# Blocked decay attention and a squared-ReLU feed-forward: block sums of the second products on VectorE with due times, all squares on ScalarE, two visits placed otherwise

## The chip, the cores and the metric

The kernel runs on one core of one Trainium2 chip. A core has TensorE (PE in the profile; its weight loads are PEld), VectorE (DVE), ScalarE (ACT), GpSimd (POOL) and SyncE (SP), which issues the transfers here. The metric is the device time of one execution in microseconds.

## The reference

Four batches of eight heads, 768 positions, head dimension 64. Attention without softmax, in blocks of 64 positions with a state; the result, 3072 tokens by 512, goes through a feed-forward of width 2048 with a squared ReLU:

```python
intra = np.einsum('bhic,bhjc->bhij', qb, kb) * Dmask[None]
intra = np.einsum('bhij,bhjd->bhid', intra, vb)
inter = np.einsum('bhid,bhde->bhie', qb * lam_pow[None], kv_state)
out[:, :, sl] = intra + inter
kv_state = lam_block[None, :, None, None] * kv_state + np.einsum('bhsd,bhse->bhde', kb_dec, vb)
...
h = np.maximum(x @ w_in, 0.0)
return (h * h @ w_out).astype(np.float32)
```

## The kernel before

**Tiles and twins.** The tokens are 24 chunks of 128. The first eight form three tiles (3, 3 and 2 chunks; `SIZES`), whose feed-forward is done step by step over 16 blocks of the width (`ffn`): every fp32 factor is split into a rounded high half and a low half, and three matmuls stand for one. The other 16 chunks form two twins of eight chunks, 512 columns wide twice. Their feed-forward multiplies 2 x 2 blocks with seven products instead of eight (a Strassen scheme in Winograd's form).

**First products.** `first_products` does, for each of eight pairs `j` of width blocks, the seven products of x with blocks of w_in; a product is six matmuls of 512 columns. ScalarE copies three of them out of PSUM (`copy`, L865), VectorE adds (`block`, L869), ScalarE applies the ReLU (L870), and the square is made on VectorE for `t == 0` (L872), on ScalarE otherwise (L874). The four results of a pair, h(t, f), are 512 columns each.

**Second products.** `second_products` goes through the seven products in the order 4, 1, 2, 6, 5, 7, 3 (`LAST_ORDER`), eight times each (a pass). Each product splits its block of h: ScalarE rounds the high half (L916), VectorE subtracts it for the low half (L917). Products 6, 5, 7 and 3 use sums of blocks; these four sums per pair are made in place on GpSimd (`add`, L923) once the earlier products have read the blocks (`sums_of`). VectorE and ScalarE collect results (L953, L956, L982). All operations of a twin's second products carry one due time, `key`, but for the splits.

**Weights.** `differences` makes the sums of weight blocks on GpSimd (L795, L804), splits them (L807 on ScalarE, L808 on VectorE) and stores them to memory; `streamed` loads 256 KB of them for each product (L844).

**Visits.** The attention of later chunks is done two chunks at a time in visits, put between the steps and products by the tables `VISITS`, `BETWEEN` (after which step of tile 2) and `INSIDE` (before which product of twin 0). A visit has a first half, an opening, a second half and another opening; between the halves a one-column copy (L684) orders the two. `PARTED` names the piece after which a visit is cut, with pieces of a step in between. After a visit, `pairs` makes sums and splits of x for the twins (L821 ScalarE, L822 VectorE; the sums at L830 on VectorE for the last pair of twin 0, on GpSimd for the others).

**What sets the order.** `Plan.order` lists all operations with a cost and a due time for each and writes out one fixed order per engine: an engine takes, of the operations that could start now, the one with the smallest due time. Each engine then works through its list in order. TensorE's order in the twins is linked by hand (`link`).

Of the kernel before, what the change touches and what calls it, by code (L numbers as in the profile page):

```python
# [226 lines left out]
PARTED = {2: 2, 5: 1}  # L227
BETWEEN = {3: 3, 4: 10, 5: 12}
# [50 lines left out]
def kernel(ctx: ExitStack, tc: tile.TileContext, ka, qv, lamx, w, out):  # L279
# [533 lines left out]
    def pairs(p, j, chunks2, key):  # L813
# [13 lines left out]
        def add(out_, a, b, op, deps):  # L827
            part = lambda c: at(c[0])[:, c[1]]
            eng, dur, fn = (("DVE", tt(256), nc.vector), ("POOL", 0.84, nc.gpsimd))[p or j < 3]
            return [plan.op(eng, dur, key, lambda: fn.tensor_tensor(out=part(out_), in0=part(a), in1=part(b), op=op), deps, [xa_, xb_])]  # L830
# [10 lines left out]
    def streamed(i, j, k, key):  # L841

        b = Buf("b")
        return b, plan.op("SP", LOAD, key - 12, lambda: nc.sync.dma_start(out=at(b).bitcast(F32), in_=kept[i][j][:, :, KEPT[k]]), stored[i, j], [b], lat=3.2)  # L844

    def first_products(p, j, key):
# [20 lines left out]
        def block(k, t, f, a, deps):  # L867
# [32 lines left out]
    def second_products(p, key):  # L900
# [6 lines left out]
        names = [f"end{k}" for k in range(4)] + ["ob9"]  # L907

# [12 lines left out]
        def add(j, out_, a, b, op, deps):  # L921
            o, a, b = ((t, 2 * j + e) for t, e in (out_, a, b))
            made[o] = [plan.op("POOL", 1.38, key, lambda: nc.gpsimd.tensor_tensor(out=at(h[o]), in0=at(h[a]), in1=at(h[b]), op=op), deps + made[a] + made[b], [h[o], h[a], h[b]])]  # L923

        def sums_of(i, j):
            if i == 4:
                add(j, (1, 1), (1, 0), (1, 1), ALU.add, read[4, j])
                add(j, (1, 0), (0, 0), (1, 0), ALU.subtract, made[1, 2 * j + 1])
            if i == 1:
                add(j, (0, 0), (1, 1), (0, 0), ALU.subtract, read[1, j] + made[1, 2 * j])  # L930
            if i == 2:
                add(j, (0, 1), (0, 1), (0, 0), ALU.subtract, read[2, j])
# [19 lines left out]
        def copies(i, dst):  # L952
            return [plan.op("ACT", act(WIDE) + 0.09, key, lambda a=a, b=b: nc.scalar.copy(at(a), at(b)), [last[i]], [a, b], uses=names) for a, b in zip(dst, banks[i])]  # L953
# [248 lines left out]
```

## Time and profile before

| | |
|---|---|
| median of 3 runs | 607.9 us (607.8 to 610.38) |
| profiled execution | 606.75 us, its span 605.0 us |
| busy, PE / PEld | 574.2 us (95%) / 471.4 us (78%) |
| busy, DVE / ACT / POOL | 470.9 us (78%) / 320.4 us (53%) / 237.7 us (39%) |
| granted clock, mean | 0.986 |
| q1 (all loads and stores) | 136.34 MB, 71.6% of 16 engines |

A busy share is an average over stages that differ. The stages, in us from the span's start: tiles 0 and 1 to about 176, tile 2 to about 249, twin 0 from 245 to 439 (first products, then from 341 second products), twin 1 from 439 to 601 (second products from 514). In a row of the timeline, equal instructions that follow each other are merged with their count; an engine is busy from the first to the last. TensorE's matmuls overlap, so a row's length is a little over the distance to the next row's start, and that distance is what one product costs.

### The profile page before, as it was taken

The numbers are of one execution on the slowest core, as the hardware profiler recorded it, in microseconds if no ns is written. First come the engines' busy times: TensorE is split into PE (matmuls) and PEld (weight loads), VectorE is DVE, ScalarE is ACT, GpSimd is POOL, SyncE is SP. The second block draws the span as 40 slices with busy tenths as digits, with TensorE's granted clock in tenths as the row PEclk, the third lists the DMA queues.
The fourth block names the chain that finished last, engine by engine and source line by source line (L and its number), as shares of the span: only waits on it lengthen the run. The fifth ranks groups of instructions, "written<-read, shape, count | busy, mean of one in ns | idle before, by whom it ended". The sixth has DMA issues, their size and how long they took to land.

```text
span 605.0 us, 12945 instructions
## 1 busy us (share of the span) xinstructions
PE 574.2 (95%) x4917; PEld 471.4 (78%) x4917; DVE 470.9 (78%) x710; ACT 320.4 (53%) x660; POOL 237.7 (39%) x198
## 2 busy tenths in 40 slices
PE   9999999999999998899989969999999999999997
PEld 7798899998878887678868757667888888666786
DVE  6998999955894879676795999998543446999755
ACT  5776677653544554457557434464345465543442
POOL 3000000042774647146662699991000002999200
PEclk9999999999998998899999979999999999999999
DMA  8999799827774692699999516566886766655765
GB/s 343 346 333 277 245 296 292 301 87 249 249 246 172 244 286 90 205 295 315 311 363 297 155 45 178 155 204 163 244 246 194 194 195 194 172 155 142 211 196 185
DMA packets 104398, 137.18 MB, mean 227 GB/s; under 512 B 7056, under 2 KB 88976, under 8 KB 104336
## 3 DMA queue, kind: packets, MB, share of 16 engines
q1 hardware_dynamic: 104192, 136.34, 71.6%
q8 instruction: 39, 0.64, 0.4%
q14 instruction: 23, 0.19, 0.1%
q10 hardware_dynamic: 144, 0.01, 0.0%
HBM read 100.67 MB, written 35.65 MB: 225 GB/s over the span
## 4 chain that ended last, share of the span: by engine, by line
PE 66%; DVE 18%; DMA 9%; issue 3%; ACT 1%; POOL 1%; SPq 1%; DVEq 0%; POOLq 0%; ACTq 0%
PE bank L469 45%; PE bank L738 9%; DVE v L917 6%; PE bank L747 4%; PE bank L744 4%; PE bank L745 4%; DMA b<-kept 3%; DMA ka<-ka 2%; DMA qv<-qv 2%; DVE gl L756 1%; DMA out<-ob 1%; DMA work<-w 1%; DVE pt L822 1%; DVE hold L553 1%; DVE h L872 1%
## 5 line engine op out<-in xcount | busy, mean ns | idle before, releaser
L469 PE MATMUL bank<-v,b 128*128 128x512 f32 x672 | 168.3, 401 | 5.6 <-DVE v L917 4.0
L469 PEld LDWEIGHTS bank<-v,b 128*128 128x128 f32 x672 | 123.1, 189 | 49.8 <-DVE v L917 25.7
L923 POOL TENSOR_TENSOR h<-h,h 128x512 f32<-128x512 f32 x64 | 105.0, 1673 | 118.8 <-DVE v L917 114.2
L917 DVE TENSOR_TENSOR v<-h,v 128x512 fp32r<-128x512 f32 x112 | 125.8, 1167 | 17.4 <-ACT v L916 13.5
L916 ACT CAST v<-h 128x512 fp32r<-128x512 f32 x112 | 67.7, 621 | 73.9 <-PE bank L469 57.5
L869 DVE TENSOR_TENSOR h<-bank,u 128x512 f32<-128x512 f32 x64 | 43.8, 690 | 63.1 <-PE bank L469 30.0
L795 POOL TENSOR_TENSOR ob<-wi 128x512 f32<-128x512 f32 x16 | 22.0, 1390 | 149.9 <-DVE xa L756 118.9
L870 ACT ACTIVATE h<-h 128x512 f32<-128x512 f32 x64 | 40.3, 632 | 33.3 <-DVE h L869 31.8
L865 ACT COPY u<-bank 128x512 f32<-128x512 f32 x48 | 27.9, 581 | 44.6 <-PE bank L469 44.6
L469 PE MATMUL bank<-ps,b 128*128 128x512 f32 x192 | 49.3, 392 | 1.7 <-ACT h L870 1.5
L469 PE MATMUL bank<-pa,b 128*128 128x512 f32 x192 | 50.4, 399 | 0.4 <-DMA b<-kept 0.2
L744 PE MATMUL bank<-wo,gh 128*128 128x512 f32 x125 | 50.3, 402 | 0.4 <-issue 0.3
L745 PE MATMUL bank<-wo,gh 128*128 128x512 f32 x125 | 49.6, 397 | 1.1 <-issue 0.9
L469 PE MATMUL bank<-pt,b 128*128 128x512 f32 x192 | 46.7, 391 | 0.0
L469 PEld LDWEIGHTS bank<-ps,b 128*128 128x128 f32 x192 | 35.7, 188 | 10.5 <-ACT h L870 1.9
L469 PEld LDWEIGHTS bank<-pa,b 128*128 128x128 f32 x192 | 36.5, 192 | 9.2 <-DMA b<-kept 1.0
L469 PEld LDWEIGHTS bank<-pt,b 128*128 128x128 f32 x192 | 35.8, 188 | 8.1 <-issue 0.5
L795 POOL TENSOR_TENSOR ob<-wo 128x512 f32<-128x512 f32 x16 | 23.3, 1462 | 38.8 <-DVE v L808 30.7
L738 PE MATMUL bank<-xb,wi 128*128 128x384 f32 x192 | 35.2, 336 | 0.0
L804 POOL TENSOR_TENSOR ob<-ob,ob 128x256 f32<-128x256 f32 x40 | 33.1, 827 | 3.1
L738 PEld LDWEIGHTS bank<-xb,wi 128*128 128x128 f32 x192 | 33.6, 188 | 0.9
L738 PE MATMUL bank<-xa,wi 128*128 128x384 f32 x180 | 34.1, 338 | 0.0
(152 smaller groups left out, 1018.3 us busy)
## 6 DMA issues: line engine op xcount, KB each, us to landing
b<-kept SPq DMA_DIRECT2D x224, 256.0 KB, 3.4
work<-w SPq DMA_DIRECT2D x32, 512.0 KB, 4.6
ka<-ka SPq DMA_DIRECT2D x24, 512.0 KB, 5.4
qv<-qv SPq DMA_DIRECT2D x20, 512.0 KB, 5.8
kept<-part SPq DMA_DIRECT2D x32, 256.0 KB, 3.6
kept<-v SPq DMA_DIRECT2D x32, 256.0 KB, 4.1
kept<-wo SPq DMA_DIRECT2D x24, 256.0 KB, 3.5
kept<-wi SPq DMA_DIRECT2D x8, 512.0 KB, 4.2
```

Source lines behind the costliest of these rows:

```text
L469: nc.tensor.matmul(*args, **kw, skip_group_check=True)
L738: nc.tensor.matmul(at(h)[:, 0:n], wt[:, cc, :], xt[:, cc, :], start=k == 0, stop=k == 3 * NCC - 1)
L744: nc.tensor.matmul(at(os_[j]), at(gh)[:, sl], woh[f], start=f == 0 and ti >= SINGLE, stop=False)
L745: nc.tensor.matmul(at(os_[j]), at(gh)[:, sl], wol[f], start=False, stop=False)
L795: prev = [plan.op("POOL", 1.38, key, lambda r=r, a=a: nc.gpsimd.tensor_tensor(out=at(r), in0=a[:, 0].bitcast(F32), in1=a[:, 1].bitcast(F32 ...
L804: o = plan.op("POOL", 0.84, key, lambda out_=out_, a=a, b=b: nc.gpsimd.tensor_tensor(out=side(out_), in0=side(a), in1=side(b), op=ALU.subt ...
L865: return plan.op("ACT", act(WIDE) + 0.09, key - 6, lambda: nc.scalar.copy(at(dst), at(banks[k])), [o], [banks[k], dst])
L869: o = plan.op("DVE", tt(WIDE) + 0.1, key - 6, lambda: nc.vector.tensor_tensor(out=at(b), in0=at(banks[k]), in1=at(a), op=ALU.add), deps, [ ...
L870: o1 = plan.op("ACT", act(WIDE) + 0.12, key, lambda: nc.scalar.activation(at(b), at(b), AF.Relu), [o], [b])
L916: oh = plan.op("ACT", act(WIDE) + 0.12, key - 12, lambda: nc.scalar.copy(rounded[hi.slot], at(b)), made[t, 2 * j + e], [b, hi], after)
L917: ol = plan.op("DVE", tt(WIDE) + 0.1, key - 12, lambda: nc.vector.tensor_tensor(out=rounded[lo.slot], in0=at(b), in1=rounded[hi.slot], op= ...
L923: made[o] = [plan.op("POOL", 1.38, key, lambda: nc.gpsimd.tensor_tensor(out=at(h[o]), in0=at(h[a]), in1=at(h[b]), op=op), deps + made[a] + ...
```

## The change

The sums of h in the second products go from GpSimd to VectorE and get due times of their own, by the product that uses them (`user`); the collecting operations get the due time at which their pass ends (`ended`). All sums of x in `pairs` go to VectorE, with later due times. All squares are made on ScalarE. Streamed loads follow each other in the order of the program (`in_turn`). The differences of w_out are due earlier, and visit 4 stands after step 9 of tile 2 instead of 10 and is cut after its first opening.

```diff
-PARTED = {2: 2, 5: 1}
-BETWEEN = {3: 3, 4: 10, 5: 12}
+PARTED = {2: 2, 4: 1, 5: 1}
+BETWEEN = {3: 3, 4: 9, 5: 12}
...
-            eng, dur, fn = (("DVE", tt(256), nc.vector), ("POOL", 0.84, nc.gpsimd))[p or j < 3]
-            return [plan.op(eng, dur, key, lambda: fn.tensor_tensor(out=part(out_), in0=part(a), in1=part(b), op=op), deps, [xa_, xb_])]
+            return [plan.op("DVE", tt(256), key, lambda: nc.vector.tensor_tensor(out=part(out_), in0=part(a), in1=part(b), op=op), deps, [xa_, xb_])]
...
-        return b, plan.op("SP", LOAD, key - 12, lambda: ...
+        return b, in_turn("streamed", plan.op("SP", LOAD, key - 12, lambda: ...
...
-            if t == 0:
-                o1 = plan.op("DVE", tt(WIDE) + 0.1, key, lambda: nc.vector.tensor_tensor(out=at(b), in0=at(b), in1=at(b), op=ALU.mult), [o1], [b])
-            else:
-                o1 = plan.op("ACT", act(WIDE) + 0.12, key, lambda: nc.scalar.activation(at(b), at(b), AF.Square), [o1], [b])
+            o1 = plan.op("ACT", act(WIDE) + 0.12, key, lambda: nc.scalar.activation(at(b), at(b), AF.Square), [o1], [b])
...
+        def ended(i):
+            return start + PASS * LAST_ORDER.index(i)
...
-        def add(j, out_, a, b, op, deps):
+        def add(j, user, out_, a, b, op, deps):
+            when = start + PASS * LAST_ORDER.index(user) + A_PROD * j - 14
             o, a, b = ((t, 2 * j + e) for t, e in (out_, a, b))
-            made[o] = [plan.op("POOL", 1.38, key, lambda: nc.gpsimd.tensor_tensor(out=at(h[o]), in0=at(h[a]), in1=at(h[b]), op=op), deps + made[a] + made[b], [h[o], h[a], h[b]])]
+            made[o] = [plan.op("DVE", tt(WIDE) + 0.1, when, lambda: nc.vector.tensor_tensor(out=at(h[o]), in0=at(h[a]), in1=at(h[b]), op=op), deps + made[a] + made[b], [h[o], h[a], h[b]])]
...
-            pairs(p - len(SIZES), j // 2, old, key if p == len(SIZES) else twice[0][1] + 4 + 12 * (j // 2))
+            pairs(p - len(SIZES), j // 2, old, begin[2] + per[2] * (11 + j / 2) if p == len(SIZES) else twice[0][1] + 30 + 8 * (j // 2))
...
-            differences(i, j, 480 + 9 * j if i == 0 else 700 + 9 * j)
+            differences(i, j, 480 + 9 * j if i == 0 else 618 + 6 * j)
```

The order that comes of it, at three places. Some line numbers are one lower in the changed program: a split's low half stands at L916, a block's addition at L868, a pair sum at L829; the sum of h is L923 in both.

VectorE, before, from the last block addition of twin 0 to the first one-column copy (L684) of the last visit; `h` are blocks of h, `v` the halves of splits, `pa` and `pz` sums of x for twin 1:

```order
L869 TENSOR_TENSOR h_0_196<-bank_58,u_214 128x512
L917 TENSOR_TENSOR v_227<-h_0_202,v_226 128x512
L917 TENSOR_TENSOR v_222<-h_0_206,v_225 128x512
L872 TENSOR_TENSOR h_0_196<-h_0_196 128x512
L917 TENSOR_TENSOR v_224<-h_0_208,v_223 128x512
L822 TENSOR_TENSOR pa<-xr_117,pa 128x4x128
L917 TENSOR_TENSOR v_227<-h_0_210,v_226 128x512
L822 TENSOR_TENSOR pz<-work,pz 128x2x128
L684 COPY small<-bank_62 128x1
```

And VectorE, changed, the same place:

```order
L923 TENSOR_TENSOR h_0_204<-h_0_203,h_0_204 128x512
L923 TENSOR_TENSOR h_0_203<-h_0_187,h_0_203 128x512
L868 TENSOR_TENSOR h_0_196<-bank_63,u_218 128x512
L916 TENSOR_TENSOR v_224<-h_0_202,v_225 128x512
L916 TENSOR_TENSOR v_226<-h_0_206,v_221 128x512
L923 TENSOR_TENSOR h_0_202<-h_0_201,h_0_202 128x512
L916 TENSOR_TENSOR v_228<-h_0_208,v_223 128x512
L923 TENSOR_TENSOR h_0_201<-h_0_185,h_0_201 128x512
L916 TENSOR_TENSOR v_225<-h_0_210,v_224 128x512
L923 TENSOR_TENSOR h_0_206<-h_0_205,h_0_206 128x512
L684 COPY small<-bank_62 128x1
```

The splits of x and the square behind the last addition are gone from here, and five sums of h (L923) stand ahead of the copy.

VectorE, before, the first splits of the second products of twin 1:

```order
L917 TENSOR_TENSOR v_227<-h_0_198,v_221 128x512
L917 TENSOR_TENSOR v_228<-h_0_200,v_223 128x512
L872 TENSOR_TENSOR h_0_195<-h_0_195 128x512
L869 TENSOR_TENSOR h_0_212<-bank_65,u_218 128x512
L869 TENSOR_TENSOR h_0_211<-bank_60,u_218 128x512
L917 TENSOR_TENSOR v_222<-h_0_204,v_224 128x512
L869 TENSOR_TENSOR h_0_196<-bank_65,u_217 128x512
L917 TENSOR_TENSOR v_227<-h_0_202,v_226 128x512
L917 TENSOR_TENSOR v_225<-h_0_206,v_221 128x512
L872 TENSOR_TENSOR h_0_196<-h_0_196 128x512
L917 TENSOR_TENSOR v_228<-h_0_208,v_223 128x512
L917 TENSOR_TENSOR v_227<-h_0_210,v_226 128x512
```

And VectorE, changed:

```order
L916 TENSOR_TENSOR v_225<-h_0_198,v_221 128x512
L916 TENSOR_TENSOR v_224<-h_0_200,v_226 128x512
L923 TENSOR_TENSOR h_0_198<-h_0_197,h_0_198 128x512
L923 TENSOR_TENSOR h_0_200<-h_0_199,h_0_200 128x512
L923 TENSOR_TENSOR h_0_197<-h_0_181,h_0_197 128x512
L923 TENSOR_TENSOR h_0_199<-h_0_183,h_0_199 128x512
L868 TENSOR_TENSOR h_0_212<-bank_65,u_214 128x512
L868 TENSOR_TENSOR h_0_211<-bank_64,u_214 128x512
L916 TENSOR_TENSOR v_223<-h_0_204,v_227 128x512
L923 TENSOR_TENSOR h_0_204<-h_0_203,h_0_204 128x512
L923 TENSOR_TENSOR h_0_203<-h_0_187,h_0_203 128x512
L868 TENSOR_TENSOR h_0_196<-bank_65,u_220 128x512
```

Four sums of h stand behind the first two splits, and then one or two ahead of each further one; the squares (L872) are gone.

TensorE, before, step 11 and the start of step 12 of tile 2 (`wi`, `wo` are weights, `gh` and `gl` the halves of h in a tile), ahead of visit 4:

```order
L738 MATMUL bank_58<-x_131,wi_77 128x256 x12
L744 MATMUL bank_60<-wo_92,gh_0_102 128x512
L745 MATMUL bank_60<-wo_92,gh_0_102 128x512
L744 MATMUL bank_65<-wo_92,gh_0_102 128x512
L745 MATMUL bank_65<-wo_92,gh_0_102 128x512
L747 MATMUL bank_60<-wo_92,gl_0_104 128x512
```

And TensorE, changed, between the two parts of visit 4; the rows on `qv`, `ka` and `work` are the visit's:

```order
L469 MATMUL bank_59<-qv_110,ka_108 64x64 x2
L744 MATMUL bank_60<-wo_92,gh_0_102 128x512
L745 MATMUL bank_60<-wo_92,gh_0_102 128x512
L744 MATMUL bank_65<-wo_92,gh_0_102 128x512
L745 MATMUL bank_65<-wo_92,gh_0_102 128x512
L738 MATMUL bank_61<-x_131,wi_77 128x256 x12
L469 MATMUL bank_58<-work,qv_111 64x64 x2
L469 MATMUL bank_63<-work 64x64 x2
```

The first part of visit 4 now stands ahead of the high halves of one step and the first product of the next, and its second part ahead of that step's low half.

## Rows read from the trace of the kernel before

**Rows 1.** Stages: span; busy PE, PEld, DVE, ACT, POOL (instructions); clock, DMA share, GB/s.
```profile
217.10:249.40 32.30, 26.59 (x597) 22.87 (x597) 30.74 (x52) 14.86 (x37) 17.75 (x18) 0.89 0.49 161
249.40:340.93 91.53, 88.35 (x1062) 71.97 (x1060) 68.70 (x113) 50.94 (x109) 48.40 (x46) 1.00 0.92 296
340.93:358.61 17.68, 11.06 (x160) 8.23 (x158) 16.72 (x18) 8.28 (x18) 14.04 (x9) 0.87 0.38 108
358.61:438.93 80.32, 77.71 (x315) 57.91 (x313) 71.74 (x75) 38.06 (x66) 49.42 (x35) 0.99 0.63 179
438.93:516.62 77.69, 77.69 (x343) 64.11 (x342) 35.33 (x51) 42.35 (x75) 5.86 (x4) 1.00 0.72 203
516.62:601.36 84.74, 82.71 (x331) 59.74 (x329) 69.67 (x64) 36.77 (x62) 47.49 (x29) 1.00 0.62 178
```

**Rows 2.** Timeline of TensorE, first products of twin 1: start, us, instruction, count.
```profile
458.14 1.52 PE L469 MATMUL bank<-ps,b 128*128 128x512 f32 x6
459.50 1.52 PE L469 MATMUL bank<-pa,b 128*128 128x512 f32 x6
```

**Rows 3.** Chain that ended last, second products of twin 0: start, us, what.
```profile
376.62 1.65 PE bank L469 x6
378.31 1.65 PE bank L469 x6
```

**Rows 4.** Timeline, second products of twin 0, GpSimd and VectorE.
```profile
364.40 28.57 POOL L923 TENSOR_TENSOR h<-h,h 128x512 f32<-128x512 f32 x17 [1.56 <-DVE v L917]
...
366.29 28.38 DVE L917 TENSOR_TENSOR v<-h,v 128x512 fp32r<-128x512 f32 x17
```

**Rows 5.** Timeline of VectorE before the twins, with GpSimd idle.
```profile
226.79 0.67 DVE L578 TENSOR_TENSOR xr<-bank,rdec 128x512 f32<-128x512 f32 x1
227.39 0.68 DVE L822 TENSOR_TENSOR ps<-xk,ps 128x512 fp32r<-128x512 f32 x1
227.99 0.41 DVE L822 TENSOR_TENSOR pz<-work,pz 128x256 fp32r<-128x256 f32 x1
228.32 0.41 DVE L553 TENSOR_TENSOR hold<-hold,small 128x256 f32<-128x256 f32 x1
```

**Rows 6.** Groups by line: count | busy us, mean ns | idle before, what ended it.
```profile
L917 DVE TENSOR_TENSOR v<-h,v 128x512 fp32r<-128x512 f32 x112 | 125.8, 1167 | 17.4 <-ACT v L916 13.5 <-PE bank L469 3.9
...
L923 POOL TENSOR_TENSOR h<-h,h 128x512 f32<-128x512 f32 x64 | 105.0, 1673 | 118.8 <-DVE v L917 114.2 <-issue 4.4
...
L872 DVE TENSOR_TENSOR h<-h 128x512 f32<-128x512 f32 x32 | 30.0, 936 | 1.4 <-ACT h L870 0.7
...
L874 ACT ACTIVATE h<-h 128x512 f32<-128x512 f32 x32 | 18.2, 616 | 0.0
...
L830 DVE TENSOR_TENSOR xk<-xk,xk 128x256 f32<-128x256 f32 x2 | 0.8, 418 | 0.0
```

**Rows 7.** Timeline of TensorE, last visit; in brackets idle time and its releaser.
```profile
349.61 0.46 PE L469 MATMUL bank<-s,qv 64*64 64x64 f32 x16
...
350.61 0.28 PE L469 MATMUL bank<-s,qv 64*64 64x64 f32 x4
355.88 0.58 PE L469 MATMUL bank<-s,qv 64*64 64x64 f32 x10 [4.99 <-DVE small L684]
```

**Rows 8.** Timeline of VectorE around the last visit.
```profile
332.44 1.29 DVE L917 TENSOR_TENSOR v<-h,v 128x512 fp32r<-128x512 f32 x2
...
350.94 1.75 DVE L822 TENSOR_TENSOR pa<-xr,pa 128x512 fp32r<-128x512 f32 x1
```

**Rows 9.** Chain that ended last: a visit and two steps of tile 2.
```profile
192.94 3.89 PE bank L469 x240
...
208.71 1.43 PE bank L738 x12
211.53 1.43 PE bank L738 x12
```

**Rows 10.** Waits of the weight loads, 210 to 250 us: us in total, times, longest.
```profile
PEld bank L747 <- DVE gl L756: 5.5, 2, 3.2
```

More of the change, by code (lines that the diff above doesn't have):

```diff
@@ L843, in streamed @@
         b = Buf("b")
-        return b, plan.op("SP", LOAD, key - 12, lambda: nc.sync.dma_start(out=at(b).bitcast(F32), in_=kept[i][j][:, :, KEPT[k]]), stored[i, j], [b], lat=3.2)
+        return b, in_turn("streamed", plan.op("SP", LOAD, key - 12, lambda: nc.sync.dma_start(out=at(b).bitcast(F32), in_=kept[i][j][:, :, KEPT[k]]), stored[i, j], [b], lat=3.2))
     def first_products(p, j, key):
@@ L898, in first_products, with second_products @@
         return run
-    def second_products(p, key):
+    def second_products(p, start):
         h, made = hidden[p], ready_h[p]
@@ L919, in splits @@
             return hi, lo, oh, ol
-        def add(j, out_, a, b, op, deps):
+        def add(j, user, out_, a, b, op, deps):
+            when = start + PASS * LAST_ORDER.index(user) + A_PROD * j - 14
             o, a, b = ((t, 2 * j + e) for t, e in (out_, a, b))
-            made[o] = [plan.op("POOL", 1.38, key, lambda: nc.gpsimd.tensor_tensor(out=at(h[o]), in0=at(h[a]), in1=at(h[b]), op=op), deps + made[a] + made[b], [h[o], h[a], h[b]])]
+            made[o] = [plan.op("DVE", tt(WIDE) + 0.1, when, lambda: nc.vector.tensor_tensor(out=at(h[o]), in0=at(h[a]), in1=at(h[b]), op=op), deps + made[a] + made[b], [h[o], h[a], h[b]])]
         def sums_of(i, j):
             if i == 4:
-                add(j, (1, 1), (1, 0), (1, 1), ALU.add, read[4, j])
-                add(j, (1, 0), (0, 0), (1, 0), ALU.subtract, made[1, 2 * j + 1])
+                add(j, 6, (1, 1), (1, 0), (1, 1), ALU.add, read[4, j])
+                add(j, 6, (1, 0), (0, 0), (1, 0), ALU.subtract, made[1, 2 * j + 1])
             if i == 1:
-                add(j, (0, 0), (1, 1), (0, 0), ALU.subtract, read[1, j] + made[1, 2 * j])
+                add(j, 6, (0, 0), (1, 1), (0, 0), ALU.subtract, read[1, j] + made[1, 2 * j])
             if i == 2:
-                add(j, (0, 1), (0, 1), (0, 0), ALU.subtract, read[2, j])
+                add(j, 3, (0, 1), (0, 1), (0, 0), ALU.subtract, read[2, j])
         def product(i, j, key):
@@ L952, in copies @@
         def copies(i, dst):
-            return [plan.op("ACT", act(WIDE) + 0.09, key, lambda a=a, b=b: nc.scalar.copy(at(a), at(b)), [last[i]], [a, b], uses=names) for a, b in zip(dst, banks[i])]
+            return [plan.op("ACT", act(WIDE) + 0.09, ended(i), lambda a=a, b=b: nc.scalar.copy(at(a), at(b)), [last[i]], [a, b], uses=names) for a, b in zip(dst, banks[i])]
         def plus(i, dst, src, deps):
-            return [plan.op("DVE", tt(WIDE) + 0.1, key, lambda a=a, b=b, c=c: nc.vector.tensor_tensor(out=at(a), in0=at(b), in1=at(c), op=ALU.add), [last[i], o] + more, [a, b, c], uses=names)
+            return [plan.op("DVE", tt(WIDE) + 0.1, ended(i), lambda a=a, b=b, c=c: nc.vector.tensor_tensor(out=at(a), in0=at(b), in1=at(c), op=ALU.add), [last[i], o] + more, [a, b, c], uses=names)
                     for a, b, c, o, more in zip(dst, banks[i], src, *deps)]
@@ L961, in store @@
                 n = N_PLAIN + 8 * p + 4 * t + 2 * d + k
-                plan.op("SP", 1.0, key, lambda a=a, n=n: nc.sync.dma_start(out=out[n], in_=at(a)), [o], [a], uses=names)
+                plan.op("SP", 1.0, start, lambda a=a, n=n: nc.sync.dma_start(out=out[n], in_=at(a)), [o], [a], uses=names)
         def after(i):
@@ L981, in after @@
                 st["r3"] = copies(7, st["a7"])
-                o4 = [plan.op("DVE", tt(WIDE), key, lambda a=a, b=b: nc.vector.tensor_tensor(out=at(a), in0=at(a), in1=at(b), op=ALU.add), [x, y], [a, b], uses=names)
+                o4 = [plan.op("DVE", tt(WIDE), ended(7), lambda a=a, b=b: nc.vector.tensor_tensor(out=at(a), in0=at(a), in1=at(b), op=ALU.add), [x, y], [a, b], uses=names)
                       for a, b, x, y in zip(st["a4"], st["a7"], st["rz"], st["r3"])]
```

## The prediction

> **What bounds the kernel now.** I read the busy times by stage first [rows 1]: TensorE's six stretches from 217.10 us on, with the count of its matmuls. In the three that belong to the second products and to the step just before the twins, VectorE is busy 30.74 of 32.30, 16.72 of 17.68, 71.74 of 80.32 and 69.67 of 84.74 us, and GpSimd is busy too; in the first products of twin 1 (438.93 to 516.62) GpSimd rests, VectorE has 35.33 of 77.69 us, and TensorE never stops. Next I took the pitch of one product. Where nothing holds TensorE, two products of six matmuls start 1.36 us apart [rows 2]; in the second products they start 1.69 us apart [rows 3]. What sets 1.69 stands in the same stretch on two other engines: 17 GpSimd sums in 28.57 us and 17 VectorE splits in 28.38 us, 1.68 and 1.67 us each, in lockstep [rows 4]. Without GpSimd beside it VectorE starts a 512-wide instruction every 0.60 us and a 256-wide one every 0.33 us [rows 5], and the means of a whole program show the same: the split (L917) 1.167 us, the square on VectorE (L872) 0.936 us, against 0.418 us for the few 256-wide pair sums that VectorE makes already [rows 6]. So the second products are paced by VectorE and GpSimd slowing each other, not by TensorE.
>
> The time above the pure matmul time, stretch by stage:
> - 516.62 to 601.36 holds 55 products: 55 x 1.36 = 74.8 of 84.74 us, so 9.9 lost.
> - 358.61 to 438.93 holds 52: 70.7 of 80.32, so 9.6 lost.
> - 340.93 to 358.61 holds 5 products (6.8) and the last visit, whose matmuls take about 3.4 (1.3 up to 350.89 [rows 7] and 2.1 in two parts behind the copies): 10.2 of 17.68, so 7.5 lost. 4.99 of it is one wait for a one-column copy on VectorE (L684) [rows 7], which stands behind a queue of instructions at up to 1.75 us each [rows 8].
> - 217.10 to 249.40: a tile-2 step costs 2.82 us, of which 1.43 is its first product, and a visit about 3.9 [rows 9]. Four first parts, five second parts (1.39), two visits and one product are 5.7 + 7.0 + 7.8 + 1.4 = 21.9 of 32.30, so 10.4 lost: waits for the low half on VectorE (L756; 5.5 us on the weight loads [rows 10]) and TensorE at a granted 0.89, that is, partly at 1.2 GHz, after its pauses [rows 1].
>
> **The change, part by part.**
>
> *Sums of second products from GpSimd to VectorE.* 64 instructions leave GpSimd (1.673 us each, 105 us [rows 6]) and 64 of 512 columns come to VectorE. Before shows none of just this sum there; its nearest rows are the 512-wide instructions with two SBUF inputs without GpSimd, 0.60 us in a row. I take 0.60, the pitch of the nearest row; the bounds are 0 (all of them in VectorE's idle time) and 1.167, the split's mean beside GpSimd; with whole spans and no overlap it is 0.69 [rows 5]. Read from the order of the changed program, VectorE has in the last four fifths of twin 0's second products (from the last L684 on) 94 wide instructions (49 splits, 21 sums, 12 pair splits, 12 others) and 24 narrow: 94 x 0.60 + 24 x 0.335 = 64.5 us, beside 70.7 us of TensorE. In twin 1 it has 67 wide ones in the first four passes: 40.2 us beside 32 x 1.36 = 43.5. Both are below TensorE, by 9% and 8%, so TensorE sets the pace again if the order is smooth: a split may run some three products ahead, and the sums mostly stand singly between two splits. Where they come in fours (the start of twin 1: 11 sums and 3 block additions among 8 splits, 22 x 0.60 = 13.2 us against 10.9) a few products wait: I leave 1.5 us lost in each twin. Gain 80.32 - 70.7 - 1.5 = 8.1 for twin 0 and 84.74 - 74.8 - 1.5 = 8.4 for twin 1.
>
> The Trainium skill speaks against this part: Perfetto Trace Analysis, Optimizing Scalar/DVE Operations, advises taking work off a saturated VectorE, even to GpSimd, and adds that the two share a port, so that it might not help. By its first half the gain above would turn into the loss priced under the second rival; by its second half, which rows 4 bear out with 1.68 us, there is nothing to lose.
>
> *The last visit.* From the first split of twin 0 to the first L684 of this visit the order now has 21 wide and 8 narrow instructions: 12.6 + 2.7 = 15.3 us from 332.44 [rows 8], the later of them waiting for a block that TensorE finishes at about 343.7 (340.93 and two products); seven wide ones and two copies stand behind that block, which makes 349. TensorE gets there at 340.93 + 6.8 + 1.2 = 348.9. The wait of 4.99 us and the 1 us before it shrink to about 1.5: 10.2 + 1.5 = 11.7 instead of 17.68, gain 6.0. Bounds: 0 (if the burst of sums ahead of the copy costs as much as the contention did) and 7.5.
>
> *Squares to ScalarE.* 32 instructions of 0.936 us leave VectorE, 32 of 0.616 [rows 6] come to ScalarE. In the first products ScalarE goes from 42.35 to 42.35 + 16 x 0.616 = 52.2 of 77.69 us (twin 1) and from 50.94 to 60.8 of 91.53 (twin 0) [rows 1]. Not on the path: cost 0, bounds 2 lost and 2 won (twin 0 loses about 6 us in that stretch now: 54 x 1.36 and three visits of 3.9 make 85.1 of 91.53; its transfers, which the change leaves as they are, are the nearest cause: 296 GB/s at a DMA share of 0.92 [rows 1]).
>
> *Pair sums to VectorE, with due times, and visit 4 a step earlier and parted.* 28 narrow sums move. 16 are counted above. The other 12 fall into the stretch before the twins: VectorE has there, from the first pair split to the first block, 20 wide and 45 narrow instructions, 27.1 us without GpSimd, where before 21 wide and 34 narrow (24.0 us by the same pitch) kept it busy for 30.74 us [rows 1]. GpSimd's 17.75 us [rows 1] shrink to one group of weight differences. Visit 4, cut in two with a step's halves between, puts 2.4 us of matmuls over the dot copies. Against it, the chunks of visit 4 are needed 2.8 us sooner, and 27.1 us is still more than the 21.9 of TensorE. I take 27.1 plus 2 for leftover contention against 32.3: gain 3.3; bounds -3 (the load late by a step) and 8.
>
> *Weight differences of w_out due earlier (618 + 6j, not 700 + 9j), and streamed loads kept in turn.* Same instructions and bytes; on GpSimd and in SP's queue the differences and their stores only move ahead a little, and six load buffers of one product each stand between a load and its use, 8 us. 0, within the 2 us above; without that cover each late load costs its delay, as a transfer hidden by nothing.
>
> Sum: 8.1 + 8.4 + 6.0 + 3.3 = 25.8. The profiled execution took 606.75 us, so 580.95; the median of the runs, 607.9, stands 1.15 above it: 582.
>
> **Rivals.**
> - *VectorE at whole spans.* Splits wait for ScalarE and sums for splits, so instructions may not follow at 0.60 but at 0.69 and 0.41. Then twin 0 needs 94 x 0.69 + 24 x 0.41 = 74.7 and twin 1's four passes 46.2: 4.0 and 2.7 more lost, and the last visit regains 3 less. 582 + 9 = 591. For it: 13.5 us of idle time ahead of the splits are ended by ScalarE [rows 6]; against: in rows 5 instructions of other kinds follow at 0.60. 22%.
> - *VectorE stays slow and becomes the bound (slower).* If the 1.167 us of the split came from something other than GpSimd (ScalarE reading the same blocks, or the transfers), 64 more wide instructions would cost as much. The point from which it decides: twin 1 has 101 wide instructions in its second products, so at 84.74 / 101 = 0.84 us each it takes as long as now, and at 1.167 it takes 118 us, 33 longer; twin 0 likewise 94 x 1.167 + 24 x 0.41 = 120, 39 longer: about 680. Against: the 0.60 of rows 5, with ScalarE and the transfers going on. 3%, most of it in milder forms around 610 to 620.
> - *The stage before the twins gets worse.* A late chunk, or pair sums ahead of the low halves: 3 lost instead of 3.3 won, and a further clock drop of 2: 590. For it: VectorE is full there in both. 15%.
> - *Nearly all is recovered.* Residuals near 0.5 in each twin, the stage at 24 and the first products 2 better: 2 + 1 + 4.5 + 2 less, 573. For it: VectorE's 8 to 9% slack; against: two visits and a burst. 12%.
> - *The change moves nothing because TensorE's own issue sets 1.69.* Excluded nearly: the same six matmuls start every 1.36 us in other stretches. Under 1%, 607.
>
> **How the numbers follow.** 47% for the forecast at 582, its own range 578 to 587; 22% and 15% for 591 and 590, 12% for 573, 4% for the slower or unchanged ones. 80% lie between 574 and 594. What a measurement of this kernel can tell from no change is about 0.5%, 3 us. Faster 0.95, same 0.02, slower 0.03.
>
> **What would show it.** Right: the splits' mean falls from 1.167 to under 0.72 us; the sums on VectorE average 0.65 to 0.70; products in both second stages start 1.36 apart but for a few; the wait for L684 is under 2 us; GpSimd's busy time falls from 237.7 us by the 105 of the sums and the time of the 28 pair sums, to some 100 to 110, and ends before the second products. Wrong: splits above 0.84 us on average; TensorE waiting for the low half of a split in most products; a wait for a chunk load at visit 4; TensorE below full clock between 217 and 250 us for longer than now.

## The result, and the profile after

The changed kernel takes 574.41 us, the median of 4 runs (572.76 to 574.97), beside 607.85 us for the kernel before in the same session (607.64 to 610.38): a ratio of 0.944, 95% interval 0.941 to 0.947. That is 33 us saved where 26 were forecast. The profiled execution took 574.97 us, with a span of 573.2; between the two profiled executions lie 31.8 us, and those can be laid out stage by stage.

The stages of the changed kernel, cut where [rows 1] is cut (the first two, the last visit, then the second products of twin 0, the first and the second of twin 1), with the same columns:

```profile
195.37:244.40 49.03, 46.12 (x726) 39.46 (x724) 42.51 (x88) 26.75 (x68) 16.91 (x17) 0.97 0.65 216
244.40:337.09 92.69, 88.21 (x1061) 72.13 (x1060) 57.54 (x107) 59.67 (x124) 40.28 (x42) 1.00 0.91 292
337.09:346.13 9.04, 9.04 (x159) 7.52 (x158) 8.67 (x17) 8.71 (x19) 0.00 (x0) 1.00 0.69 183
346.13:416.99 70.86, 70.86 (x319) 58.67 (x314) 64.76 (x116) 38.34 (x67) 0.00 (x0) 1.00 0.71 202
416.99:494.55 77.56, 77.56 (x344) 64.19 (x343) 27.70 (x42) 50.99 (x90) 0.00 (x0) 1.00 0.73 208
494.55:569.51 74.96, 74.96 (x331) 61.75 (x329) 57.23 (x90) 37.10 (x63) 0.00 (x0) 1.00 0.69 201
```

From 337 us on TensorE's busy time equals the stretch: nothing holds it any more. GpSimd has no instruction there; over the whole program its busy time fell from 237.7 to 101.4 us. VectorE does more instructions than before (116 and 90, against 75 and 64) in less busy time. 70.86 us for 52 products and 74.96 for 55 are 1.363 us each, the unhindered pitch of [rows 2].

| Stage | before | after | gained | forecast |
|---|---|---|---|---|
| up to the end of visit 3 | 196.83 | 195.37 | 1.5 | none |
| from there to the end of twin 0's first product | 52.58 | 49.03 | 3.6 | 3.3 |
| other first products of twin 0 | 91.52 | 92.69 | -1.2 | 0 ± 2 |
| products around the last visit, and it | 17.68 | 9.04 | 8.6 | 6.0 |
| second products of twin 0 | 80.32 | 70.86 | 9.5 | 8.1 |
| first products of twin 1 | 77.69 | 77.56 | 0.1 | 0 |
| second products of twin 1 | 84.74 | 74.96 | 9.8 | 8.4 |

The groups that answer to [rows 6], in the same columns:

```profile
L916 DVE TENSOR_TENSOR v<-h,v 128x512 fp32r<-128x512 f32 x112 | 75.0, 689 | 18.7 <-ACT v L915 10.4
...
L869 ACT ACTIVATE h<-h 128x512 f32<-128x512 f32 x64 | 40.4, 633 | 24.4 <-DVE h L868 21.8
...
L923 DVE TENSOR_TENSOR h<-h,h 128x512 f32<-128x512 f32 x64 | 43.0, 686 | 0.1
...
L870 ACT ACTIVATE h<-h 128x512 f32<-128x512 f32 x64 | 38.4, 624 | 0.4
```

The split (now L916) fell from 1167 to 689 ns and the sum (L923), now on VectorE, takes 686. Splits and sums together cost VectorE 118.0 us, less than the 125.8 of the splits alone before. All three figures (split, sum and GpSimd's 101.4 us) are signs that the prediction named for being right.

VectorE in the middle of twin 0's second products, start and duration in us:

```profile
359.36 0.69 DVE L916 TENSOR_TENSOR v<-h,v 128x512 fp32r<-128x512 f32 x1
359.97 0.69 DVE L923 TENSOR_TENSOR h<-h,h 128x512 f32<-128x512 f32 x1
360.57 0.69 DVE L916 TENSOR_TENSOR v<-h,v 128x512 fp32r<-128x512 f32 x1
361.18 0.68 DVE L923 TENSOR_TENSOR h<-h,h 128x512 f32<-128x512 f32 x1
```

Starts lie 0.60 to 0.61 us apart: the pitch of [rows 5] holds for splits and sums in turn, and the whole span of 0.69 is not what counts.

The last visit, TensorE first and then VectorE, which answers to [rows 7, 8]:

```profile
339.81 4.24 PE L469 MATMUL bank<-v,b 128*128 128x512 f32 x18
343.99 0.46 PE L469 MATMUL bank<-s,qv 64*64 64x64 f32 x16
...
346.13 2.11 PE L469 MATMUL bank<-v,b 128*128 128x512 f32 x8
```

```profile
344.23 0.69 DVE L923 TENSOR_TENSOR h<-h,h 128x512 f32<-128x512 f32 x1
344.83 0.15 DVE L684 COPY small<-bank 128x1 f32<-128x1 f32 x1
345.24 0.16 DVE L684 COPY small<-bank 128x1 f32<-128x1 f32 x1 [0.26 <-PE bank L469]
```

The visit's matmuls take 2.14 us (343.99 to 346.13) without a pause. The one-column copy comes in time, and for the second copy VectorE waits for TensorE, not the other way.

What TensorE still waits for between 195 and 346 us (us in total, times, longest); behind 346 the view has no row:

```profile
PE bank L469 <- issue: 3.0, 5, 1.1
PE bank L747 <- DVE gl L756: 2.6, 2, 2.0
PE bank L469 <- DMA b<-kept: 1.6, 3, 1.1
```

### The profile page after: what moved, and what is told of

Same layout as the page of the kernel before. It is cut to its first block, busy times and chain, and to the rows that moved or that the text cites. A ratio compares the mean times of both kernels' runs of the same rounds, so it can differ in the third digit from the quotient of the medians.

```text
span 573.2 us, 12887 instructions
## 1 busy us (share of the span) xinstructions
PE 554.7 (97%) x4917; PEld 470.9 (82%) x4917; DVE 421.4 (74%) x770; ACT 339.0 (59%) x692; POOL 101.4 (18%) x106
## 4 chain that ended last, share of the span: by engine, by line
PE 76%; DMA 9%; DVE 8%; issue 2%; POOL 2%; ACT 1%; SPq 0%; DVEq 0%; ACTq 0%
PE bank L469 54%; PE bank L738 11%; PE bank L747 4%; DMA ka<-ka 4%; PE bank L744 4%; PE bank L745 4%; DMA b<-kept 2%; DMA qv<-qv 2%; DMA kept<-part 1%; POOL ob L804 1%; DVE gl L756 1%; DVE hold L545 1%; POOL ob L795 1%; DVE work L554 1%; DVE hold L553 1%
## 5 line engine op out<-in xcount | busy, mean ns | idle before, releaser
L469 PE MATMUL bank<-v,b 128*128 128x512 f32 x672 | 153.3, 389 | 0.0
L469 PEld LDWEIGHTS bank<-v,b 128*128 128x128 f32 x672 | 126.0, 188 | 26.2
L868 DVE TENSOR_TENSOR h<-bank,u 128x512 f32<-128x512 f32 x64 | 44.2, 691 | 76.3 <-ACT u L864 38.5
L916 DVE TENSOR_TENSOR v<-h,v 128x512 fp32r<-128x512 f32 x112 | 75.0, 689 | 18.7 <-ACT v L915 10.4
L869 ACT ACTIVATE h<-h 128x512 f32<-128x512 f32 x64 | 40.4, 633 | 24.4 <-DVE h L868 21.8
L795 POOL TENSOR_TENSOR ob<-wi 128x512 f32<-128x512 f32 x16 | 22.6, 1423 | 148.8 <-DVE xa L756 118.0
L923 DVE TENSOR_TENSOR h<-h,h 128x512 f32<-128x512 f32 x64 | 43.0, 686 | 0.1
L870 ACT ACTIVATE h<-h 128x512 f32<-128x512 f32 x64 | 38.4, 624 | 0.4
L804 POOL TENSOR_TENSOR ob<-ob,ob 128x256 f32<-128x256 f32 x40 | 32.3, 809 | 3.1
```

What stands on the lines that cost most here:

```text
L469: nc.tensor.matmul(*args, **kw, skip_group_check=True)
L795: prev = [plan.op("POOL", 1.38, key, lambda r=r, a=a: nc.gpsimd.tensor_tensor(out=at(r), in0=a[:, 0].bitcast(F32), in1=a[:, 1].bitcast(F32 ...
L804: o = plan.op("POOL", 0.84, key, lambda out_=out_, a=a, b=b: nc.gpsimd.tensor_tensor(out=side(out_), in0=side(a), in1=side(b), op=ALU.subt ...
L868: o = plan.op("DVE", tt(WIDE) + 0.1, key - 6, lambda: nc.vector.tensor_tensor(out=at(b), in0=at(banks[k]), in1=at(a), op=ALU.add), deps, [ ...
L916: ol = plan.op("DVE", tt(WIDE) + 0.1, key - 12, lambda: nc.vector.tensor_tensor(out=rounded[lo.slot], in0=at(b), in1=rounded[hi.slot], op= ...
L923: made[o] = [plan.op("DVE", tt(WIDE) + 0.1, when, lambda: nc.vector.tensor_tensor(out=at(h[o]), in0=at(h[a]), in1=at(h[b]), op=op), deps + ...
```

## The experiments

Times are medians with the range of the runs; ratios are to the kernel before, with their 95% intervals. In the diffs + is the kernel tried.

**The sums alone, and all but the sums.** First the changed kernel with its sums back on GpSimd:

```
- plan.op("DVE", tt(WIDE) + 0.1, when, ... nc.vector.tensor_tensor(...
+ plan.op("POOL", 1.38, when, ... nc.gpsimd.tensor_tensor(...
```

> The changed kernel with one part undone: the 64 sums of h in the second products go back to GpSimd, with their new due times and everything else as changed. Theory A (GpSimd and VectorE slow each other, and that alone made the 1.69 us product): both second products go back to about 1.69 us per product while sums run, the last visit waits again; 574.4 + 9 + 9 + 5 = 597 us, between 590 and 603; the split's mean goes back above 1.0 us. Theory B (due times, squares and pairs did it): 574 to 578 us, the split stays near 0.69 us.

605.9 us (603.13 to 609.01, 10 runs), 0.998 [0.995, 1.000]: theory A in kind, but 3 us above its range. The second products of both twins in it, columns of [rows 1]:

```profile
350.64:438.87 88.23, 78.32 (x315) 61.62 (x314) 71.62 (x91) 37.61 (x66) 31.08 (x20) 0.93 0.56 161
516.38:599.86 83.48, 81.43 (x331) 60.03 (x329) 68.37 (x63) 37.23 (x63) 46.23 (x28) 1.00 0.62 181
```

The rest of the change brings TensorE out of the last visit 8 us sooner (350.64 instead of 358.61), and twin 0's second products, which then hold VectorE's pair sums beside GpSimd's sums, take 88.2 instead of 80.3 us and eat that up.

Next the kernel before with nothing but the sums moved to VectorE, with the due times of the change (`when = key + PASS * LAST_ORDER.index(user) + A_PROD * j - 14`):

> The kernel before with one part of the change alone: the 64 sums of h on VectorE with the new due times; squares, pair sums, visits and the other due times as before. Theory A: it brings most of the 33 us; twin 1's second products take about 75 to 76 us (84.7 before), twin 0's about 73 (80.3; the pair sums of twin 1 still run on GpSimd beside it), the last visit regains about 5; total 583 to 590 us. Theory B (only all parts together): above 595 us.

585.17 us (583.18 to 586.83), 0.962 [0.958, 0.966]. Twin 1's second products reach the unhindered pace by this edit alone, and twin 0's lose most of their excess:

```profile
348.26:424.68 76.42, 73.61 (x317) 59.58 (x314) 67.45 (x102) 38.29 (x66) 16.47 (x15) 0.98 0.65 190
502.78:577.74 74.96, 74.96 (x331) 61.77 (x329) 58.77 (x92) 36.68 (x62) 0.00 (x0) 1.00 0.68 201
```

So, beside the kernel before in the same session (607.48 us), the sums are worth 22 us alone and the rest 2 without them; both together are worth 33. The 9 us between need both. A part of them is the pair sums, which here still stand on GpSimd (16.47 us of it in twin 0) and are tried alone further on; the rest is not taken apart.

**What makes VectorE slow: GpSimd's reads.** The changed kernel and 32 idle additions on GpSimd, in and out of blocks that nobody reads:

```
+ spare = [Buf("ka"), Buf("qv")]
...
+ if p == 1 and len(products) <= 32:
+     plan.op("POOL", 1.38, key, lambda: nc.gpsimd.tensor_tensor(out=at(spare[1])[:, 0], in0=at(spare[0])[:, 0], in1=at(spare[0])[:, 1], op=ALU.add), [o], spare)
```

> The changed kernel with 32 idle additions on GpSimd in twin 1's second products, one after each of the first 32 products: 512 columns, two inputs in SBUF, buffers that nothing else uses by then, and no one waits for them. The output stays the reference's. Theory A (the two engines slow each other whatever GpSimd adds): each addition slows one VectorE instruction by about 1.07 us (1.67 - 0.60), 34 us over the first four passes, where VectorE has 40 us of its own and TensorE 43.5: that stretch takes about 74 us, total about 600 us, between 588 and 606. Rival E (the loss before came from splits waiting for sums made on another engine): 574 to 575 us. By the Trainium skill, SBUF — State Buffer, Who interferes with whom, a VectorE instruction with two SBUF inputs contends with a GpSimd instruction that reads SBUF: as theory A.

601.79 us (600.3 to 602.88), 0.991 [0.988, 0.994]. Theory A holds, though in another stretch than expected: as they waited for no data, the additions ran at 332 to 385 us, beside the last visit and twin 0's second products and not in twin 1. The groups of that stretch:

```profile
L952 POOL TENSOR_TENSOR qv<-ka 128x512 f32<-128x512 f32 x32 | 50.6, 1582 | 17.3 <-DMA b<-kept 14.8
```

```profile
L925 DVE TENSOR_TENSOR h<-h,h 128x512 f32<-128x512 f32 x16 | 24.6, 1545 | 0.1
L918 DVE TENSOR_TENSOR v<-h,v 128x512 fp32r<-128x512 f32 x13 | 21.0, 1630 | 0.0
L868 DVE TENSOR_TENSOR h<-bank,u 128x512 f32<-128x512 f32 x3 | 2.0, 676 | 0.0
```

GpSimd starts an addition every 1.66 us (53.04 for 32), VectorE's splits and sums take 1.5 to 1.6 us until it stops, and 0.68 after. The loss is 27 us by the medians and 25 between the profiled executions, some 0.8 us for each addition, whose result nothing waits for. L868, with one input in PSUM, is not slowed.

The same with memsets, which write only:

```
+     plan.op("POOL", 1.38, key, lambda: nc.gpsimd.memset(at(spare[1])[:, 0], 0.0), [o], spare)
```

> The same as the run before it, but GpSimd's 32 additions are memsets of 512 columns: it writes SBUF and reads nothing. The output stays the reference's. Theory A1 (what is shared is the reading side): 574 to 575 us, VectorE's instructions stay at 0.69 us. Theory A2 (any GpSimd access to SBUF holds VectorE up): as with the additions, 585 us and more. By the Trainium skill, SBUF — State Buffer, Who interferes with whom, a GpSimd instruction that only writes does not contend with a VectorE instruction of two SBUF inputs: as A1.

575.09 us (571.35 to 578.68), 0.947 [0.941, 0.952], the time of the changed kernel, as theory A1 had it. 32 memsets run beside the same instructions, which stay at their pace:

```profile
L952 POOL MEMSET qv<- 128x512 f32 x32 | 16.9, 527 | 17.5 <-PE bank L469 15.8
```

```profile
L925 DVE TENSOR_TENSOR h<-h,h 128x512 f32<-128x512 f32 x13 | 8.7, 684 | 0.1
L918 DVE TENSOR_TENSOR v<-h,v 128x512 fp32r<-128x512 f32 x8 | 5.4, 684 | 0.0
```

Then the additions held to twin 1, the first of them reading the last hidden block in one kernel and an early split in the other:

```
+     plan.op("POOL", 1.38, key, ... in0=at(late) if first else ..., [o] + (made[0, NF - 1] if first else []), spare + [late] * first)
```

```
+     plan.op("POOL", 1.38, key, ... in0=rounded[hi.slot].bitcast(F32) if first else ..., [o] + [oh] * first, spare + [hi] * first)
```

> The idle additions once more, now in twin 1. In the earlier run nothing but the written order held them back, so GpSimd made all 32 from 332 us on, beside the last visit and twin 0's second products, and cost 26 us there. Here the first of them reads the last block of h that twin 1's first products make, so that all 32 run beside twin 1's second products, where no visit and no sums of x are. The output stays the reference's. Theory A: 32 x about 0.8 us as there, less what VectorE's slack of 3 us in the first four passes covers: 593 to 601 us, TensorE's 55 products take 95 to 102 us instead of 75.0, and twin 0 stays at its 70.9. If contention needs the visits or the pair sums: 574 to 577 us.

> The changed kernel and 32 more GpSimd additions of 512 columns on blocks that nobody reads, the first of which waits for a split early in twin 1's second products; the output is complete. Theory A (contention: what GpSimd reads beside VectorE costs VectorE, whatever GpSimd computes): twin 1's 55 second products take 100 to 106 us instead of 75, VectorE's and GpSimd's instructions go at 1.67 to 1.68 us in lockstep while the additions run, twin 0 stays at 71: 600 to 607. Theory B (the additions cost by order or by waits of the second products for GpSimd, which there are none of here): 573 to 577.

605.92 us (603.28 to 609.21, 10 runs), 0.997 [0.995, 0.999], and 603.8 us (603.61 to 604.61), 0.992 [0.990, 0.993]. Both kernels write a wrong output, though the expectations call it complete. Why is open, and I read from them the engines' pace alone. Twin 1's second products, from the first split, take 106.62 us in the second of them, against 77.7, while twin 0's keep their 70.87:

```profile
492.58:599.20 106.62, 83.31 (x343) 64.58 (x341) 90.92 (x99) 39.50 (x67) 46.73 (x30) 0.97 0.51 147
```

That is 29 us, 0.9 for each addition. So the loss follows GpSimd's additions from one twin to the other.

**Pair sums back on GpSimd.** Their own due times as before:

```
- return [plan.op("DVE", tt(256), key, ... nc.vector.tensor_tensor(...
+ eng, dur, fn = (("DVE", tt(256), nc.vector), ("POOL", 0.84, nc.gpsimd))[p or j < 3]
+ return [plan.op(eng, dur, key, ... fn.tensor_tensor(...
```

> The changed kernel with the 28 pair sums of x back on GpSimd and their due times as before; the sums of h stay on VectorE. Theory A: 16 sums beside twin 0's second products slow 16 to 20 VectorE instructions by 0.8 us, 12 more before the twins; 2 to 4 us lost in the stage before the twins and 2 to 6 in twin 0: 578 to 584 us. Rival (VectorE has the room for it): 574 to 575 us.

582.64 us (580.36 to 583.6), 0.959 [0.955, 0.962]: the pair sums' move is worth 8 us by the medians. In the profiled execution 6.4 us are lost by the visit among twin 0's first products, which starts at 260.78, not 254.36. But visit 3 already starts 2.9 us later there (194.36, not 191.48), and up to visit 3 each engine has the same order in both kernels. That leaves 3.5 us to the pair sums in this stage, where TensorE waits for the low half, L756, longer than in the rows above (2.6 us):

```profile
PE bank L747 <- DVE gl L756: 6.2, 3, 4.8
```

Another 0.6 is lost in the last visit and 2.3 in twin 0's second products (73.20 us).

**The placement of the visits**, as before:

```
+ PARTED = {2: 2, 5: 1}
+ BETWEEN = {3: 3, 4: 10, 5: 12}
```

> The changed kernel with visit 4 after step 10 of tile 2 again and not parted. By the prediction's term the stage before the twins gains about 3.3 us from pair sums and visits together. If the visit carries it: 576 to 578 us. If the pair sums on VectorE and GpSimd's rest carry it: 573.5 to 575 us.

573.46 us (571.71 to 576.83), 0.945 [0.940, 0.950]: no difference from the changed kernel that can be told, so the visit does not carry the gain.

**The due times of the sums and of what follows a pass:**

```
- return start + PASS * LAST_ORDER.index(i)
+ return start
- when = start + PASS * LAST_ORDER.index(user) + A_PROD * j - 14
+ when = start
```

> The changed kernel, but the sums of h and the collecting operations all carry the start of the second products as due time. In the order all 32 sums of a twin now stand among its first 16 splits: 48 instructions at 0.60 make 28.8 us beside 16 products of 1.36, 21.8 us; a lead of three products (4 us) covers a part. Theory C (a place for each sum is needed): 2 to 4 us lost in each twin, total 578 to 583 us. Theory D (VectorE's sum over the stage is all that counts): 574 to 575 us.

577.01 us (573.37 to 579.15), 0.948 [0.943, 0.954]; twin 0's second products take 70.85 us and twin 1's 75.56. That is at most 0.6 us in these stretches, not the 2 to 4 in each twin of theory C. The total lies between both theories, and its interval overlaps that of the changed kernel.

**Squares of the first half back on VectorE:**

```
+ if t == 0:
+     o1 = plan.op("DVE", tt(WIDE) + 0.1, key, ... op=ALU.mult), [o1], [b])
+ else:
      o1 = plan.op("ACT", act(WIDE) + 0.12, key, ... AF.Square), [o1], [b])
```

> The changed kernel with the 32 squares of t == 0 back on VectorE. Without GpSimd's sums each costs 0.60 to 0.69 us there, and in the first products VectorE has room (in twin 1 it was busy for 35 of 78 us with them). Theory A: 574 to 577 us, at most 2 us lost around the last visit, where two squares stand ahead of the one-column copy. Rival (the squares on ScalarE carry a part of the gain): 580 us and more.

578.08 us (575.8 to 581.8), 0.951 [0.947, 0.956], between what theory A and the rival had. By the medians the move is worth 3.7 us, but the intervals of this kernel and the changed one just touch. Twin 0's first products, cut as in the stage table, take 95.9 us instead of 92.7.

**More work to VectorE.** The weights' sums and differences on GpSimd (L795 and L804) went to VectorE too, those of w_out in one kernel, all in the other:

```
- plan.op("POOL", 1.38, key, ... nc.gpsimd.tensor_tensor(
+ eng, wide, narrow, fn = ("DVE", tt(WIDE) + 0.1, tt(256), nc.vector) if i == 1 else ("POOL", 1.38, 0.84, nc.gpsimd)
+ plan.op(eng, wide, key, ... fn.tensor_tensor(
```

> A step further than the change: the sums of w_out's weight blocks (16 wide, 32 narrow) too go from GpSimd to VectorE. In twin 0's first products VectorE was busy 57.5 of 92.7 us beside GpSimd's 40.3; 16 x 0.60 + 32 x 0.335 = 20 us come to it, and what it does beside GpSimd gets shorter by some 10. Theory A (contention is what costs): 572 to 575 us, since that stage's losses of about 7 us are mostly waits for transfers. Rival (VectorE is late for block additions then): 577 us and more.

> All sums of weight blocks on VectorE, of w_in as well, so that GpSimd adds nothing any more after the tables at the start. Before 249 us VectorE is the fullest engine beside TensorE (42.5 of 49.0 us in the last stage before the twins); 40 us of instructions come in there and before, 16.9 us of GpSimd beside that stage go. Theory A with VectorE's sum as the limit: 573 to 580 us. Rival (GpSimd's part had been free there): above 582 us.

580.94 us (578.51 to 582.48), 0.956 [0.953, 0.959], and 582.27 us (580.51 to 584.14), 0.958 [0.955, 0.961]: both 6 to 8 us longer than the changed kernel, so theory A fell in both. Twin 0's first products take 96.6 us in the first and 98.9 in the second instead of 92.7; the second also reaches visit 3 only at 198.35 instead of 191.48 us. Moving work off GpSimd does not pay everywhere. I read this as: it pays where TensorE waits for the two slowed engines, and not where VectorE would become late. No run tests that reading further.

**The weight differences, due as late as before:**

```
- differences(i, j, 480 + 9 * j if i == 0 else 618 + 6 * j)
+ differences(i, j, 480 + 9 * j if i == 0 else 700 + 9 * j)
```

> The changed kernel with the differences of w_out due at 700 + 9j as before. The prediction put this edit at 0, within 2 us: 573 to 577 us. Rival (stores that are due late hold up the streamed loads of twin 0's second products): 578 us and more, with TensorE waiting for loads after 340 us.

599.78 us (598.68 to 600.42), 0.987 [0.985, 0.989]: far outside, as the rival had it. Nearly all of the 25 us is one wait in twin 0's second products; first TensorE, then SP's queue:

```profile
PE bank L469 <- DMA b<-kept: 22.7, 1, 22.7
```

```profile
SPq L785 <- DVE v L808: 27.9, 4, 26.9
```

A store (L785) waits for the low half of the last weight difference (L808 on VectorE), the streamed load behind it in SP's queue waits with it, and TensorE for the load. Six load buffers cover 8 us, not 27. Why does this cost nothing in the kernel before, whose due times are these? There the stores wait little:

```profile
SPq L785 <- DVE v L808: 3.4, 4, 1.3
```

Two more runs asked why.

> The changed kernel with the 28 pair sums back on GpSimd and the weight differences of w_out due as late as before (700 + 9j): both edits back together. Alone, the first made it 8 us longer, the second 25. Theory A (the late due time is costly because the pair sums and sums of hidden blocks now stand ahead of the last difference on VectorE; with the pair sums gone about half of that queue is gone): 582 to 595, less than 10 us on top of the 582.6 of the pair sums alone. Theory B (the two are independent): about 607, with a wait of some 23 us for a streamed chunk in twin 0's second products.

Pair sums on GpSimd as above together with the late due time: 601.0 us (599.31 to 602.47), 0.987 [0.985, 0.989], with a wait of 20.7 us at the same place. The late due time still costs 18 us more than the pair sums on GpSimd alone (582.64 us), which is neither theory's price, but the wait is theory B's: the pair sums are not the cause.

> The changed kernel with the weight differences of w_out due as late as before (700 + 9j) and the squares of the first 512 columns back on VectorE. Alone, the late due time gave 599.8 and the squares 578.1. Theory C (the late due time costs only because squares on ScalarE let the sums of the hidden blocks come earlier in VectorE's order and pass the last weight difference; with the squares on VectorE the last L808 is instruction 499, ahead of the first sum at 516, not 562 behind 75 others): 576 to 582, no wait of a streamed load over 4 us in twin 0's second products. Theory D (the due time costs by itself, whatever the squares): 597 or more with a wait of some 20 us there.

Squares of the first half on VectorE together with the late due time: 577.12 us (573.8 to 578.5), 0.948 [0.942, 0.954], and the long wait is gone, as theory C had it:

```profile
SPq L785 <- DVE v L808: 3.3, 6, 1.1
```

Number of an instruction in VectorE's planned order, the last L808 and the first sum of hidden blocks (the blocks of h):

```
                                     last L808   first sum
changed kernel                             484         491
late due time                              562         487
late, pair sums on GpSimd                  535         475
late, squares on VectorE                   499         516
before with the sums moved (due late)      487         504
```

With the squares on VectorE the sums, which need squared blocks, are planned behind the last weight difference whatever its due time. With the squares on ScalarE they come earlier and pass it, unless it is due sooner.

> The changed kernel without the order that streamed loads are kept in. Theory A (the order only fixes what SP does anyway): 573 to 577, first products of twin 0 within 1.5 us of 92.7. Theory B (the order is what keeps a late load from blocking others; without it TensorE waits for chunks): 580 or more, with waits of the chunk loads longer than 3 us on TensorE.

Without `in_turn` around the streamed loads: 576.07 us (575.08 to 577.04), 0.946 [0.944, 0.948]; no difference that can be told, with the early due time. With the late one it was not tried.

> The changed kernel with the weight differences of w_out due at 606 + 5j instead of 618 + 6j. Theory A (once the last difference is ahead of the sums of the hidden blocks, more lead is worth nothing): 572 to 577. Theory B (the loads' waits that are left in twin 0's first products, 1.6 us, come from these differences): 571 to 573 and the first products of twin 0 at 91 us or less.

Weight differences sooner still, 606 + 5j: 578.94 us (576.59 to 579.64), 0.949 [0.947, 0.952]. The wait for loads fell from 1.6 to 0.8 us, but TensorE now waits 2.0 us for VectorE's L518 in the same stretch. Both theories missed the time. It does not show that sooner is worse: 3.1 of the 4.5 us stand already at visit 3 (194.63 instead of 191.48), up to which nothing is changed. None of the kernels is faster than the changed one beyond its interval.

## Why the prediction was right in kind and too small in size

The mechanism was right. The step that failed is the size of the losses left over: 1.5 us in each twin and 1.5 around the last visit were put in, and 0.2, 0.2 and none were measured; beside them, the last visit's matmuls were taken as 3.4 us and measure 2.14. One more step, the cover of the weight differences, came out at its 0 for a wrong reason.

- *Lockstep of VectorE and GpSimd sets 1.69 us a product* [rows 3, 4]: right, and shown by the additions that no other work waits for, by the memsets, and by the sums alone.
- *0.60 us for a sum on VectorE* [rows 5]: right. The rival with whole spans, 0.69 us, fell, and so did a VectorE that stays slow.
- *1.5 us left in each twin* for sums in fours and dense stretches: wrong. 70.86 - 70.7 and 74.96 - 74.8 are 0.2 each. VectorE is busy 91% of twin 0's stretch and TensorE still never waits, which fits a lead of three products that takes up every burst. 2.8 us of the miss.
- *The last visit, 6.0 of at most 7.5*: mis-sized by 2.6 us. Its matmuls were taken as 3.4 us, from records that lay partly in the half-clock stretch after the wait; undisturbed they take 2.14. So 8.7 us were lost there before, not 7.5, and the remaining wait of 1.5 was not there either. The stretch behind the wait in the kernel before, columns of [rows 1], stands at a granted clock of 0.50, that is, at 1.2 GHz:

```profile
355.88:358.61 2.73, 2.18 (x61) 1.88 (x61) 2.73 (x3) 0.00 (x0) 2.68 (x2) 0.50 0.02 6
```

- *The stage before the twins, 3.3*: 3.6 came, but for one of the reasons only, so that the number fits so well is partly luck. It hangs on the pair sums: with them on GpSimd, 3.5 us more are lost there. The visit's new place, argued at length, did nothing that can be told.
- *Squares 0, bounds 2 lost and 2 won*: not settled. The run has 3.7 us won by the medians, above the bound, with intervals that just touch. In the stage table there is no gain, and twin 0's first products became 1.2 us longer.
- *Weight differences due earlier 0, hidden by six load buffers*: the reason was wrong. The cover holds 8 us, the delay would have been 27: this edit repairs what another one, the squares' move, does to the order. I costed each against the order of before, where the last difference stands ahead of the sums even when these are moved (487 and 504 in the table). That the term still came out at 0 is luck: the change had both edits.
- *Loads in turn 0*: right as far as was tried.
- Beyond the terms: 1.5 us come before visit 3, where nothing was changed. Visit 3 starts between 191.1 and 196.7 us in the profiled executions of the kernels that have the same order up to there (all but the one with all weight sums on VectorE), so I read this as spread between executions. And the median of the changed kernel lies 0.6 us under its profiled execution, that of before 1.1 above: another 1.7 us between the forecast and the medians.

- *The rival "nearly all is recovered", 573 at 12%*: it came nearest in time, but not by its own terms. Its two largest, the stage before the twins at 24 us (4.5 less) and first products 2 us better, did not come; the last visit and the spread stood in for them.

The misses add up: 1.4 + 1.4 + 2.6 + 0.3 - 1.2 + 0.1 + 1.5 + 1.7 = 7.8 us, beside 33.4 - 25.9 = 7.5. 3.2 of them (1.5 and 1.7) are spread that no step could have foreseen. More than half is one habit: leaving a loss for bursts in each of three places (1.4, 1.4 and 1.5 us), without a row that shows one.

## What to carry to other kernels

When two engines run in lockstep at a pace that neither has alone, price the work by moving it onto either of them at the undisturbed pitch: the one that takes it over can end up with less busy time than before. Check such a price on a small edit first, since the same step with the weights' sums did not pay. Before costing an edit of due times at nothing, look in the new order at what would stand ahead of the instruction without that edit, since edits of one change may need each other. And a residue that is put in for caution needs its own row, as any other term.

## What was not expected of the hardware

VectorE slows beside GpSimd by where its inputs lie, not by being VectorE. In the kernel before, the group means of twin 1's second products hint at it:

```profile
L917 DVE TENSOR_TENSOR v<-h,v 128x512 fp32r<-128x512 f32 x53 | 61.9, 1214 | 11.7 <-ACT v L916 9.1 <-PE bank L469 2.6
L956 DVE TENSOR_TENSOR end<-bank,end 128x512 f32<-128x512 f32 x8 | 5.3, 684 | 3.0 <-PE bank L469 3.0
```

The split, with both inputs in SBUF, takes 1214 ns on average; an addition of the same shape with one input in a PSUM bank takes 684. But GpSimd's sums fill only a part of that stretch, and of the eight additions only two ran beside them (676 and 673 ns). The first run with idle additions shows it on one line of the program, with GpSimd adding all the time (332 to 385 us):

```profile
L554 DVE TENSOR_TENSOR s<-work,mask 128x256 f32<-128x256 f32 x1 | 1.5, 1511 | 0.0
L554 DVE TENSOR_TENSOR s<-bank,mask 128x256 f32<-128x256 f32 x2 | 0.7, 404 | 0.0
```

With `work` and `mask`, both in SBUF, it takes 1511 ns; with a bank in place of `work`, 404. The Trainium skill (SBUF — State Buffer, Who interferes with whom) says that a VectorE instruction with two SBUF inputs contends with GpSimd's reads and not with its writes, and that one with at most one SBUF input, outside the two-port modes, does not contend; both halves agree with the rows here, the memsets (splits at 684 ns) and L554. What the runs add is the price. Where VectorE paces the products, each 512-column addition on GpSimd cost the kernel 0.8 to 0.9 us. And VectorE's own delay is nearly the same for a short instruction as for a long one: 256 columns take 1.51 us for 0.41 [rows 5], 512 columns up to 1.75 [rows 8] for 0.69, about 1.1 us more each.
